# Four loads moved in time or to another queue, and attention sums moved to GpSimd, in an attention kernel with two dense layers

## The chip, the cores and the metric

The kernel runs on one core of a Trainium2 chip. The metric is the device time of one execution in microseconds (us); lower is better. The core has a matrix engine (TensorE, PE in the profile, with its weight loads as PEld), VectorE (DVE), ScalarE (ACT), GpSimd (POOL) and SyncE (SP), which here only issues transfers. Transfers run on 16 DMA engines that the core's queues share.

## What is computed

```python
a = np.exp(phi - np.max(phi, axis=2, keepdims=True))          # phi: batch 8, heads 8, seq 576, 32 memories
a = a / (np.sum(a, axis=2, keepdims=True) + 1e-09)
k_m = np.einsum('bhsm,bhsd->bhmd', a, k)                      # k, v, q: 8 x 8 x 576 x 64
v_m = np.einsum('bhsm,bhsd->bhmd', a, v)
scores = np.matmul(q, k_m.transpose(0, 1, 3, 2)) / np.sqrt(64)
scores = np.exp(scores - np.max(scores, axis=-1, keepdims=True))
attn = scores / (np.sum(scores, axis=-1, keepdims=True) + 1e-09)
x = np.matmul(attn, v_m).transpose(0, 2, 1, 3).reshape(4608, 512)
h = x @ moe_w_in                                              # 512 x 2048, weights given as float64
x = (h - np.tanh(h)) @ moe_w_out                              # 2048 x 512
h = x @ moe2_w_in
out = np.where(h > 0, h, np.exp(np.minimum(h, 0)) - 1) @ moe2_w_out
```

## The kernel before

The program is unrolled and every engine works its instructions in the order in which the Python code emits them; waits on other engines and on transfers are put in for each data dependence and for each reuse of a tile. What is emitted early on an engine and has to wait therefore holds all that is emitted behind it on that engine.

**Attention** is cut into 16 units (one batch, four heads). `Attention.unit` (line 108) is a generator; each `yield` ends a stage. In the order of its stages: maximum of phi over the sequence (119), its transpose and spread (122 to 131), the subtraction (132), exp into `a` (137), the sum of `a` over its six chunks (140, VectorE), matmuls of `a` with k and v into `km` together with the sums (147, 150), transposes of q (171), scores (192), their maximum, exp and sum (197 to 204), the normalising product (205), a transpose into `pT` (208), a split into a high and a low float part `phl` (212, 213), and a store of the result, called P, to DRAM (219). `eng` is VectorE for units 0 and 1 and GpSimd for the others. Stages also issue the next unit's loads (98 to 105) on SyncE's queue.

**Weights** come as float64. `conv` (511) loads one quarter of a weight block (512 KB, tile `raw`, two buffers) by SyncE's queue, and one stage later `convert` takes |w| of the high words on ScalarE (48, into one PSUM buffer), then two and two operations on VectorE (50, 51 and 54, 55), a copy on ScalarE (58) and a difference on GpSimd (60). Weights of layer 2 are then stored to DRAM as float32 pairs (539).

**`Staged`** runs such generators side by side: `round()` starts a waiting generator when its time has come and takes one stage of each live one, older ones first. `units` holds the attention units (one starts every six rounds), `cv` the conversions (one every two or three rounds). `need()` (507) takes rounds of `cv` at once until a weight is there.

**The stages of the program.** First (line 576) rounds of `units`, and from round 9 also of `cv`, until units 0 and 1 are done. Then 64 blocks (665) of layer 1: a block is one group of 288 tokens for one quarter of the hidden width, with two steps (`i` = 0, 1). A step emits `h_unit` (12 matmuls that read P and `vw`, 318), `g_a` (four ScalarE operations, 329 to 332), `g_b` (GpSimd 337, VectorE 338), `g_d` of the step before (350, 351), stores of finished x (378), one `x_unit` (12 matmuls, 363, and a copy to an x tile, 370 or 372), a round of `cv` and one of `units`, in every fourth block the products `vw` (303 to 308), a second `x_unit`, `g_c` (VectorE 343, 344), and a second round of `units` (in blocks 0 to 6, 28 and 29 also of `cv`). At the top of a block, P of the next block is loaded from DRAM by SyncE's queue into one of two buffers (711, 290). Layer 2 (72 groups of work on lines 419 and 456) follows and keeps its weights on the chip.

The lines that matter here, as the profile numbers them:

## Time and profile before

| | us |
|---|---|
| median of three runs (1793.1 to 1796.35) | 1793.4 |
| the profiled execution | 1789.79 |
| its span, from first to last instruction | 1787.6 |

| engine | busy us | share of the span |
|---|---|---|
| PE | 1613.6 | 90% |
| PEld | 1483.2 | 83% |
| DVE | 1255.0 | 70% |
| ACT | 959.1 | 54% |
| POOL | 763.8 | 43% |

The mean granted clock of TensorE is 0.973 of full speed. A busy share is an average over stages with different limits; the rows below are therefore cut by stage. Blocks begin at about 78 us, units are done at about 453 us, layer 1 ends at about 985 us.

### The profile page before, as it was taken

The numbers are of one execution on the slowest core, as the hardware profiler recorded it, in microseconds if no ns is written. First come the engines' busy times: TensorE is split into PE (matmuls) and PEld (weight loads), VectorE is DVE, ScalarE is ACT, GpSimd is POOL, SyncE is SP. The second block draws the span as 40 slices with busy tenths as digits, with TensorE's granted clock in tenths as the row PEclk, the third lists the DMA queues.
The fourth block names the chain that finished last, engine by engine and source line by source line (L and its number), as shares of the span: only waits on it lengthen the run. The fifth ranks groups of instructions, "written<-read, shape, count | busy, mean of one in ns | idle before, by whom it ended". The sixth has DMA issues, their size and how long they took to land.

```text
span 1787.6 us, 30091 instructions
## 1 busy us (share of the span) xinstructions
PE 1613.6 (90%) x11496; PEld 1483.2 (83%) x11496; DVE 1255.0 (70%) x1805; ACT 959.1 (54%) x1713; POOL 763.8 (43%) x539
## 2 busy tenths in 40 slices
PE   4547787888898999898999999999999999999998
PEld 2336777778897999898999999999999999999997
DVE  5859887988788998888875555555555555555554
ACT  2436776777887887787875333333333333333332
POOL 2235655656665665566653222222222222222222
PEclk9758999999999999999999999999999999999999
DMA  9547577675455445555557621111121121211210
GB/s 214 165 118 191 157 204 215 198 224 181 170 167 168 153 168 190 205 198 205 188 189 276 249 61 57 59 59 58 55 62 58 59 59 57 60 57 59 60 36 24
DMA packets 140934, 238.40 MB, mean 133 GB/s; under 512 B 8184, under 2 KB 102392, under 8 KB 138744
## 3 DMA queue, kind: packets, MB, share of 16 engines
q1 hardware_dynamic: 140792, 236.49, 42.5%
q8 instruction: 91, 1.49, 0.4%
q14 instruction: 51, 0.42, 0.1%
HBM read 159.78 MB, written 75.50 MB: 132 GB/s over the span
## 4 chain that ended last, share of the span: by engine, by line
PE 62%; DVE 13%; DMA 12%; ACT 6%; issue 5%; POOL 2%; SPq 1%; DVEq 0%; ACTq 0%; POOLq 0%
PE h_ps L419 23%; PE o_ps L456 22%; PE x_ps L363 9%; PE h_ps L318 5%; DMA p<-p_dram 5%; DMA raw<-in_moe_w_in_dram 2%; DVE s L343 2%; DVE vw L308 2%; DMA q<-in_q_dram 1%; DMA raw<-in_moe_w_out_dram 1%; DVE h_ps L338 1%; DMA x_dram<-x 1%; ACT t L329 1%; PE vw_ps L303 1%; POOL g L351 1%
## 5 line engine op out<-in xcount | busy, mean ns | idle before, releaser
L363 PE MATMUL x_ps<-g,w 128*128 128x288 f32 x3072 | 448.7, 299 | 40.3 <-DVE vw L308 16.7
L363 PEld LDWEIGHTS x_ps<-g,w 128*128 128x128 f32 x3072 | 422.3, 190 | 52.1 <-ACT x L370 14.7
L419 PEld LDWEIGHTS h_ps<-x,wi 128*128 128x128 f32 x3456 | 429.7, 190 | 11.7
L445 POOL TENSOR_TENSOR e<-hm,e 128x512 fp32r<-128x512 f32 x144 | 186.5, 1295 | 587.3 <-ACT e L444 443.3
L419 PE MATMUL h_ps<-x,wi 128*128 128x256 f32 x3456 | 433.2, 281 | 0.0
L456 PE MATMUL o_ps<-wo,e 128*128 128x512 f32 x1728 | 423.8, 394 | 0.7 <-POOL e L445 0.7
L456 PEld LDWEIGHTS o_ps<-wo,e 128*128 128x128 f32 x1728 | 314.8, 188 | 65.0 <-POOL e L445 1.1
L430 ACT ACTIVATE t_ps<-hm 128x512 f32<-128x512 f32 x144 | 86.7, 602 | 514.3 <-DVE hm L429 514.3
L337 POOL TENSOR_TENSOR v<-t,u 128x576 f32<-128x576 f32 x128 | 183.2, 1431 | 269.2 <-ACT u L330 221.6
L318 PE MATMUL h_ps<-p,vw 128*128 128x288 f32 x1536 | 236.6, 304 | 28.4 <-DMA p<-p_dram 25.2
L318 PEld LDWEIGHTS h_ps<-p,vw 128*128 128x128 f32 x1536 | 217.1, 194 | 33.0 <-issue 24.0
L436 DVE SCALAR_TENSOR_TENSOR hm<-hm,t_ps 128x512 f32<-128x512 f32 x144 | 99.0, 688 | 200.6 <-ACT hm L431 200.6
L351 POOL TENSOR_TENSOR g<-s,g 128x576 fp32r<-128x576 f32 x128 | 183.9, 1437 | 77.0 <-ACT g L350 69.5
L429 DVE TENSOR_SCALAR hm<-h_ps 128x512 f32<-128x512 f32 x144 | 99.6, 692 | 139.0 <-PE h_ps L419 139.0
L343 DVE SCALAR_TENSOR_TENSOR s<-s,v 128x576 f32<-128x576 f32 x128 | 156.5, 1223 | 0.8 <-POOL v L337 0.7
L329 ACT ACTIVATE t<-h_ps 128x576 f32<-128x576 f32 x128 | 83.0, 648 | 90.6 <-issue 43.0
L338 DVE TENSOR_TENSOR h_ps<-h_ps,t 128x576 f32<-128x576 f32 x128 | 98.3, 768 | 35.4 <-ACT u L330 34.4
L344 DVE COPY_PREDICATED s<-big,h_ps 128x576 f32<-128x576 uint32 x128 | 106.6, 833 | 11.0
L308 DVE TENSOR_TENSOR vw<-vw_ps,vw 64x512 fp32r<-64x512 f32 x128 | 88.0, 687 | 36.5 <-ACT vw L306 34.4
L332 ACT ACTIVATE big<-u,bias 128x576 f32<-128x576 f32 x128 | 98.1, 767 | 11.4 <-DVE s L344 11.2
L438 DVE TENSOR_TENSOR hm<-hm,h_ps 128x512 f32<-128x512 f32 x144 | 99.0, 687 | 5.0
L437 DVE SCALAR_TENSOR_TENSOR hm<-hm,t_ps 128x512 f32<-128x512 f32 x144 | 99.0, 687 | 5.0
(86 smaller groups left out, 1776.1 us busy)
## 6 DMA issues: line engine op xcount, KB each, us to landing
x_dram<-x SPq DMA_DIRECT2D x128, 288.0 KB
xr<-x_dram SPq DMA_DIRECT2D x72, 512.0 KB
p<-p_dram SPq DMA_DIRECT2D x62, 576.0 KB
raw<-in_moe_w_in_dram SPq DMA_DIRECT2D x32, 512.0 KB
raw<-in_moe_w_out_dram SPq DMA_DIRECT2D x32, 512.0 KB
w_dram<-wst SPq DMA_DIRECT2D x32, 512.0 KB
kv<-in_k_dram SPq DMA_DIRECT2D x16, 576.0 KB
kv<-in_v_dram SPq DMA_DIRECT2D x16, 576.0 KB
```

What stands on the lines that cost most here:

```text
L308: nc.vector.tensor_tensor(lo, src, r32(hi), op=ALU.subtract)
L318: nc.tensor.matmul(ps[:, j, :NB], lhsT=vw[a][:, kc, 128 * j:128 * j + 128], rhs=p[:, kc, b, :], start=(k == 0), stop=(k == 5))
L329: nc.scalar.activation(t, w[0], ACTF.Tanh)
L337: nc.gpsimd.tensor_tensor(v, t, u, op=ALU.mult)
L338: nc.vector.tensor_tensor(h, h, t, op=ALU.subtract)
L343: nc.vector.scalar_tensor_tensor(s, s, G_B, v, op0=ALU.add, op1=ALU.mult)
L344: nc.vector.copy_predicated(s, big.bitcast(U32), d)
L351: nc.gpsimd.tensor_tensor(g[:, 1], s, r32(g[:, 0]), op=ALU.subtract)
L363: nc.tensor.matmul(ps, lhsT=wo[pg][:, a, j, 128 * dm:128 * dm + 128], rhs=g[:, b, j, :], start=(k == 0), stop=(k == 11))
L419: nc.tensor.matmul(ps[:, j], lhsT=w3[:, a, kc, 128 * j:128 * j + 128], rhs=x[:, b, kc, :], start=(k == 0), stop=(k == 11))
L445: nc.gpsimd.tensor_tensor(e[:, 1], hm, r32(e[:, 0]), op=ALU.subtract)
L456: nc.tensor.matmul(self.acc[n][tg], lhsT=e[:, a, j, 128 * tg:128 * tg + 128], rhs=w4[:, b, j, :], start=(pg == 0 and j == 0 and i == 0), s ...
```

## The change

- P is loaded two blocks ahead by ScalarE's queue, in the second step of a block between `g_a` and `g_b`, if the units it comes from are done by then; if not, at the top of the block before its own by SyncE's queue, as it was.
- x tiles have four buffers in place of three, `raw` three in place of two; `s` of the gate has two in place of three, the conversions' `a` two in place of three, the small attention tiles two in place of three. `dmax` takes the place of `pT`, and the partial sums of `a` that of `phl`.
- The sum of `a` over its six chunks is three GpSimd additions (384, 128 and 128 elements per partition) in place of one VectorE reduction. The normalising product and the low part of P of units 0 and 1 are also on GpSimd now.
- The first three weight quarters are loaded right behind the loads of units 0 and 1 and converted three rounds apart; `cv` rounds begin at round 7, units 2 and 3 start one round later.
- A later conversion is loaded two rounds earlier ahead of its |w|, and |w| is emitted on its own, by `half()`, after `g_c` or at the start of the next round.

```diff
@@ -73,7 +73,7 @@
         pool = lambda name, n: ctx.enter_context(
             tc.tile_pool(name=name + side, bufs=n, side=side, reuse_waits="tile"))
         self.wk = pool("at_wk", 1)
-        self.sm = pool("at_sm", 3)
+        self.sm = pool("at_sm", 2)
         self.sc_p = pool("at_sc", 2 if side == "left" else 1)
         self.ps = psum
         self.q_p = pool("at_q", 2)
@@ -122,7 +122,7 @@
         nc.tensor.transpose(mT, cmax.rearrange("p h m -> p (h m)"), ident[:96, :96])
         nmax = sm.tile([128, 1], F32, tag="nmax", name="nmax")
         nc.vector.tensor_reduce(nmax, mT, axis=AX.X, op=ALU.max)
-        dmax = wk.tile([128, 128], F32, tag="dmax", name="dmax")
+        dmax = wk.tile([128, S], F32, tag="pT", name="dmax")[:, :128]
         nc.vector.tensor_scalar(dmax, ident, nmax, None, op0=ALU.mult)
         yield
         bmax = ps_tile([96, 4, M], "bmax")
@@ -137,7 +137,11 @@
         nc.scalar.activation(a[:96].rearrange("p c h m -> p h c m"), ph, ACTF.Exp)
         self.load(nxt, "phi")
         yield
-        nc.vector.tensor_reduce(asum[:96], a[:96].rearrange("p c h m -> p h m c"), axis=AX.X, op=ALU.add)
+        part = r32(wk.tile([128, 2, 2, NB], F32R, tag="phl", name="asum3")).rearrange("p r t s -> p (r t s)")
+        part = part[:96, :12 * M].rearrange("p (c h m) -> p c h m", c=3, h=4)
+        nc.gpsimd.tensor_tensor(part, a[:96, 0:3], a[:96, 3:6], op=ALU.add)
+        nc.gpsimd.tensor_tensor(part[:, 0], part[:, 0], part[:, 1], op=ALU.add)
+        nc.gpsimd.tensor_tensor(asum[:96], part[:, 0], part[:, 2], op=ALU.add)
         yield
         self.loaded.pop((u, "kv"))
         km = ps_tile([128, 2 * D + 2], "km")
@@ -202,7 +206,7 @@
         nc.vector.tensor_reduce(smax, s, axis=AX.X, op=ALU.add)
         nc.vector.tensor_scalar(smax, smax, GUARD, None, op0=ALU.add)
         nc.vector.reciprocal(smax, smax)
-        eng.tensor_tensor(s, s, smax.to_broadcast([128, 18, M]), op=ALU.mult)
+        nc.gpsimd.tensor_tensor(s, s, smax.to_broadcast([128, 18, M]), op=ALU.mult)
         yield
         pT = wk.tile([128, S], F32, tag="pT", name="pT")
         nc.vector.transpose(pT, s.rearrange("p j m -> p (j m)"))
@@ -210,7 +214,7 @@
         phl = wk.tile([128, 2, 2, NB], F32R, tag="phl", name="phl")
         pTv = pT.rearrange("p (r s) -> p r s", r=2)
         nc.scalar.activation(phl[:, :, 0], pTv, ACTF.Copy)
-        eng.tensor_tensor(phl[:, :, 1], pTv, r32(phl[:, :, 0]), op=ALU.subtract)
+        nc.gpsimd.tensor_tensor(phl[:, :, 1], pTv, r32(phl[:, :, 0]), op=ALU.subtract)
         yield
         for c, t in enumerate(first_p or ()):
             for hq in range(2):
@@ -242,12 +246,13 @@
     def __init__(self, gens=(), every=1):
         self.todo, self.live, self.every, self.wait = deque(gens), [], every, 0
         self.timed, self.rounds = deque(), 0
-        self.first = deque()
+        self.first, self.apart = deque(), []
 
     def at(self, rnd, gen):
         self.timed.append((rnd, gen))
 
     def round(self):
+        self.half()
         while self.timed and self.timed[0][0] <= self.rounds:
             self.live.append(self.timed.popleft()[1])
         self.rounds += 1
@@ -256,9 +261,18 @@
         if self.wait <= 0 and (self.first or self.todo):
             self.live.append((self.first or self.todo).popleft())
             self.wait = self.every
-        for g in list(self.live):
+        self.step([g for g in self.live if g not in self.apart])
+
+    def half(self):
+
+        gens, self.apart = self.apart, []
+        self.step(gens)
+
+    def step(self, gens):
+        for g in gens:
             try:
-                next(g)
+                if next(g):
+                    self.apart.append(g)
             except StopIteration:
                 self.live.remove(g)
 
@@ -274,9 +288,9 @@
         self.tc, self.nc, self.const = tc, tc.nc, const
         self.p_dram, self.x2_dram = p_dram, x2_dram
         pool = lambda name, n, **kw: ctx.enter_context(tc.tile_pool(name=name, bufs=n, reuse_waits="tile", **kw))
-        self.x_p = pool("x2", 3)
+        self.x_p = pool("x2", 4)
         self.g_p = pool("g", 5)
-        self.gw, self.gw1 = pool("gw", 3), pool("gw1", 1)
+        self.gw, self.gw1 = pool("gw", 2), pool("gw1", 1)
         self.p_p = pool("p", 2)
         self.vw_p = pool("vw", 1)
         self.vw, self.p, self.g, self.x2, self.work, self.x2_pool = {}, {}, {}, {}, {}, {}
@@ -285,9 +299,9 @@
         self.p[sw, n] = self.p_p.tile([128, 2, 2, NB], F32R, tag="p", name="p")
         return self.p[sw, n]
 
-    def load_p(self, sw, n):
+    def load_p(self, sw, n, queue):
         t = self.new_p(sw, n)
-        self.nc.sync.dma_start(out=r32(t).rearrange("p r t s -> p (r t s)"),
+        queue.dma_start(out=r32(t).rearrange("p r t s -> p (r t s)"),
                                in_=self.p_dram[n // 2, :, :, n % 2].rearrange("g q m f -> (g q) m f"))
 
     def vw_half(self, vm, wi, pg, po, pars=(0, 1)):
@@ -492,8 +506,8 @@
         m1 = Moe1(tc, l1a, const, p_dram, x2_dram)
         wt_p = {0: new(l1b, "wt0", 1, side="right")}
         vm_p = new(l1b, "vm", 2, side="right")
-        cv_p = new(l1b, "cv", 3, side="right")
-        raw_p = new(l1b, "raw", 2, side="right")
+        cv_p = new(l1b, "cv", 2, side="right")
+        raw_p = new(l1b, "raw", 3, side="right")
         wst_p = []
         misc = m1.misc = new(top, "ps_m", 3, space=PSUM)
         cv_ps = new(top, "ps_c", 1, space=PSUM)
@@ -508,7 +522,7 @@
             while not all((1, kind, pg, c) in converted for c in range(2)):
                 cv.round()
 
-        def conv(layer, kind, pg, c):
+        def conv(layer, kind, pg, c, lead=2):
 
             w = {("i", 1): w1, ("o", 1): w2, ("i", 2): w3, ("o", 2): w4}[kind, layer]
             raw = raw_p.tile([128, 512], mybir.dt.int64, tag="raw", name="raw")
@@ -518,7 +532,8 @@
             else:
                 r0 = 256 * pg + 128 * c
                 nc.sync.dma_start(out=raw, in_=w[r0:r0 + 128, :])
-            yield
+            for k in range(lead + 1):
+                yield k == lead
             staged = []
 
             def dst():
@@ -551,11 +566,15 @@
         at0.p_done = at1.p_done = p_done = set()
         new_vm(0)
         nc.vector.memset(r32(vm[0]), 0.0)
-        cv = Staged(conv_l1("i", 0, 1) + conv_l1("o", 0, 1), 2)
         for what in "phi", "kv", "q0", "q1":
             at0.load(0, what)
             at1.load(1, what)
-        cv.round()
+        cv_first = [conv(1, "i", k // 2, k % 2, 0) for k in range(3)]
+        cv = Staged([conv(1, "i", 1, 1)] + conv_l1("o", 0, 1), 2)
+        cv.wait = 7
+        for k, g in enumerate(cv_first):
+            next(g)
+            cv.at(3 * k, g)
 
         def unit(u):
             if u % 4 == 0 and u:
@@ -569,13 +588,13 @@
 
         first_p = [m1.new_p(0, n) for n in range(2)]
         units = Staged()
-        for u, t in ((0, 0), (1, 1), (2, 8), (3, 9)):
+        for u, t in ((0, 0), (1, 1), (2, 9), (3, 10)):
             units.at(t, unit(u))
         for u in range(4, 2 * B):
             units.at(19 + 6 * (u - 4), unit(u))
         while 1 not in p_done:
             units.round()
-            if units.rounds >= 9:
+            if units.rounds >= 7:
                 cv.round()
         pro.close()
         m1.ps_h = new(ps_h_ctx, "ps_h", 2, space=PSUM)
@@ -708,11 +727,16 @@
             if ss == 1 and j == 1 and sub == 1 and bp + 1 < B // 2 or bi == 29:
                 load_vm((bp + 1) % (B // 2))
             if nxt and nxt not in m1.p:
-                m1.load_p(*nxt)
+                m1.load_p(*nxt, nc.sync)
             for i in range(2):
                 pg = 2 * sw + i
                 m1.h_unit(sw, n, pg)
                 m1.g_a(n, pg)
+                if i == 1 and bi + 2 < len(blocks):
+                    a_ss, a_bp, a_sub, a_j = blocks[bi + 2]
+                    after = (2 * a_ss + a_sub, 4 * a_bp + a_j)
+                    if all(u in p_done for u in range(2 * (after[1] // 2) + 2)):
+                        m1.load_p(*after, nc.scalar)
                 m1.g_b(n, pg)
                 if pend:
                     m1.g_d(*pend.pop())
@@ -732,8 +756,10 @@
                     soon.popleft()()
                 x_next(bi < 22)
                 m1.g_c(n, pg)
+                cv.half()
                 if bi < 7 or 28 <= bi < 30:
                     cv.round()
+                    cv.half()
                 units.round()
                 if vw_next:
                     m1.vw_half(vm[vbp], wi[vpg + i], vpg + i, 1, pars)
```

## Rows read from the trace of the kernel before

**Rows 1.** Stage windows: length, engines' busy us (instructions), granted clock, DMA share, GB/s.

```profile
147.00:501.00 354.00, 298.21 (x2554) 271.01 (x2553) 298.31 (x442) 260.29 (x506) 205.94 (x139) 0.97 0.64 191
...
501.00:985.00 484.00, 445.38 (x3275) 437.55 (x3274) 402.23 (x558) 372.30 (x642) 291.53 (x202) 0.99 0.57 192
...
985.00:1788.00 803.00, 797.11 (x5083) 721.07 (x5081) 457.11 (x633) 273.17 (x459) 224.03 (x159) 1.00 0.21 66
```

**Rows 2.** Waits: who waited for whom: us in total, times, longest.

```profile
ACT cv_m L48 <- DMA raw<-in_moe_w_in_dram: 30.4, 4, 12.5
...
ACT cv_m L48 <- DMA raw<-in_moe_w_out_dram: 8.8, 2, 6.4
...
PE h_ps L318 <- DMA p<-p_dram: 25.2, 16, 5.8
...
DVE x L372 <- DMA x_dram<-x: 23.3, 14, 2.6
...
PE km L150 <- DVE asum L140: 15.9, 10, 3.6
```

**Rows 3.** Timeline, 26 to 43 us: start, length, instruction, idle before and releaser.

```profile
26.20 1.26 SPq L517 DMA_DIRECT2D raw<-in_moe_w_in_dram  x1
...
41.60 0.62 ACT L48 ACTIVATE cv_m<-raw 128x512 f32<-128x512 f32 x1 [12.46 <-DMA raw<-in_moe_w_in_dram]
...
42.60 0.29 PEld L192 LDWEIGHTS sc<-qT,kT 128*64 128x64 f32 x2 [10.48 <-ACT qT L173]
```

**Rows 4.** Timeline, 112 to 126 us.

```profile
112.30 0.67 SPq L290 DMA_DIRECT2D p<-p_dram  x1
...
113.47 0.91 SPq L517 DMA_DIRECT2D raw<-in_moe_w_in_dram  x2
...
125.59 0.62 ACT L48 ACTIVATE cv_m<-raw 128x512 f32<-128x512 f32 x1 [12.17 <-DMA raw<-in_moe_w_in_dram]
```

**Rows 5.** Timeline: the first ScalarE operation of blocks 24, 32 and 36.

```profile
501.38 0.65 ACT L329 ACTIVATE t<-h_ps 128x576 f32<-128x576 f32 x1 [0.46 <-issue]
...
598.96 0.65 ACT L329 ACTIVATE t<-h_ps 128x576 f32<-128x576 f32 x1 [0.46 <-issue]
...
642.27 0.65 ACT L329 ACTIVATE t<-h_ps 128x576 f32<-128x576 f32 x1 [0.46 <-issue]
```

**Rows 6.** Windows: blocks 32 to 35, blocks 44 to 47, and one microsecond.

```profile
599.00:642.30 43.30, 41.73 (x315) 41.31 (x314) 40.25 (x57) 37.37 (x65) 28.93 (x20) 1.00 0.47 159
...
735.60:781.60 46.00, 42.17 (x314) 41.36 (x313) 39.74 (x57) 37.22 (x64) 28.87 (x20) 1.00 0.59 205
...
621.00:622.00 1.00, 1.00 (x9) 1.00 (x8) 0.97 (x3) 0.70 (x2) 0.52 (x1) 1.00 0.24 97
```

**Rows 7.** Line 290, its issue times, and the timeline of one late P.

```profile
L290 SPq DMA_DIRECT2D p<-p_dram x62: 531/538/811, 112.3 to 934.2; - x62
...
660.31 0.79 SPq L290 DMA_DIRECT2D p<-p_dram  x1
...
671.98 0.58 PE L318 MATMUL h_ps<-p,vw 128*128 128x288 f32 x1 [2.26 <-DMA p<-p_dram]
```

**Rows 8.** Groups by form (busy us, mean ns | idle before), L343's min/median/max ns.

```profile
L140 DVE TENSOR_REDUCE asum<-a 96x128 f32<-96x768 f32 x16 | 23.6, 1475 | 0.0
...
L205 POOL TENSOR_TENSOR s<-s,smax 128x576 f32<-128x576 f32 x14 | 17.8, 1269 | 11.5 <-DVE smax L204 9.4 <-DVE rs L156 2.1
...
L132 POOL TENSOR_TENSOR phi<-phi,bm 96x768 f32<-96x768 f32 x14 | 28.8, 2055 | 36.0 <-ACT bm L131 32.8 <-DVE cv_m L51 3.3
...
L205 DVE TENSOR_TENSOR s<-s,smax 128x576 f32<-128x576 f32 x2 | 1.5, 758 | 0.1
...
L343 DVE SCALAR_TENSOR_TENSOR s<-s,v x128: 736/1258/2395, 81.8 to 961.0; 128x576 f32<-128x576 f32 x128
```

**Rows 9.** ScalarE's last gate operation, and line 378's issue times (min/median/max ns).

```profile
L332 ACT ACTIVATE big<-u,bias 128x576 f32<-128x576 f32 x128 | 98.1, 767 | 11.4 <-DVE s L344 11.2
...
L378 SPq DMA_DIRECT2D x_dram<-x x128: 354/365/3339, 150.7 to 977.7; - x128
```

## What the change should do to the time

> **What bounds the kernel now.** I first cut the span into stages, because the busy shares of the page are an average. In layer 2 the matrix engine works 797 of 803 us [rows 1]; the change touches nothing there, so all that can move lies in the first 985 us. In blocks 2 to 23 (147 to 501 us) no engine is full: PE and DVE are each busy 84% of the time (298 of 354 us), and 16% goes to waits. In blocks 24 to 63 PE is busy 92% (445 of 484 us).
>
> Then I read the waits [rows 2] for those that the change names, and the timeline for where they lie. ScalarE waited 39.2 us in six places for the float64 weights of a conversion (30.4 + 8.8). Two of the six are 12 us long and stop everything: the weights issued at 26.20 us reach ScalarE at 41.60, and PE, idle for 10.48 us, waits for a ScalarE copy queued behind that |w| [rows 3]; the pair issued at 113.47 ends a wait of 12.17 us at 125.59 [rows 4]. PE waited 25.2 us in 16 places for P, and VectorE 23.3 us in 14 places for a free x tile.
>
> Last I measured the block. From the start of block 32 to that of block 36 are 642.27 - 598.96 = 43.3 us [rows 5], in which PE is busy 41.7 [rows 6]; I take this for the floor that PE sets for four blocks. Blocks 44 to 47 take 46.0 for the same matmuls. The eight blocks from 24 take 501.38 to 598.96, 97.6 us, against 86.6 at the floor. What differs is the transfers: a DMA share of 0.59 in place of 0.47 [rows 6]. P of block 38 was issued at 660.31 and PE could begin only at 671.98 [rows 7], 11.7 us later, while a block lasts 43.3 / 4 = 10.8.
>
> One row explains why P is slow. While P alone is moving, the DMA share is 0.24 at 97 GB/s [rows 6]: P runs on a quarter of the engines, four of 16. Its 590 KB (128 rows of 4608 bytes) take 590 / 97 = 6.1 us of each of those four. For blocks 44 to 47 I work out an estimate: all engines together are busy 0.59 x 46.0 x 16 = 434 us, four loads of P take 4 x 4 x 6.1 = 98 of it, the other 336 spread over 16 engines are 21.0 each, so the four engines have 21.0 + 24.4 = 45.4 us of work in 46.0. Likewise blocks 32 to 35 give 38.7 of 43.3, and blocks 2 to 23 (22 loads, share 0.64 of 354) give 193 + 134 = 327 of 354.
>
> **The change part by part.** I count gains against the profiled execution (1789.8 us; span 1787.6, so 2.2 lie around it).
>
> *First weights early.* The wait of rows 3 exists since the second quarter is issued at 26.20, behind eight loads of units 2 and 3. Now three quarters go out ahead of those. PE got back 10.48 there; the bytes do not shrink, k and v of units 2 and 3 land some 1.0 MB later (two more quarters at about 240 GB/s, an estimate, 4 us), and the first |w| now stands earlier, so that it may itself wait 1 to 3 us. I take **7 us**, bounds 3 and 10.5.
>
> *Products of units 0 and 1 to GpSimd, sums of a there too, in the prologue.* DVE loses four operations of 0.758 and, for units 2 and 3, two sums of 1.475 [rows 8], 6.0 us. On GpSimd a product takes 1.27, so each step of a unit's own chain is 0.5 us longer. I count half, **3 us**, bounds -2 and 6. Units 2 and 3 start one round later and block 1 must force one more round: **-1 us**.
>
> *|w| issued apart, two rounds more lead.* At 113 us the lead is spent: block 1 needs the first output weights and takes three rounds of conversions at once, in which the new load's two rounds pass; and its transfer still stands behind P of block 2, issued at 112.30 after a wait for the store of unit 3 (it cannot go early, since unit 3 is not done). But one x unit, its copy and some GpSimd work now come ahead of that |w|. I take **5 us** of the 12.17, bounds 0 and 12. The other four waits, 39.2 - 12.46 - 12.17 = 14.6 us, lie in ordinary steps, where two rounds are two steps of about 5 to 8 us; with the one step that it had, that is more than the 15 us that the load of rows 3 took. I take **9 us**, since part of such a wait is not PE's, bounds 4 and 14.6. The |w| stands behind `g_c` of the same step and ahead of the next `t`; only the VectorE operations of a later round read it. This costs nothing as long as the weights are there; if not, `t` of the next step waits instead, as now.
>
> *Sum of a on GpSimd.* Units 5 to 15 have it in the blocks: VectorE loses 11 x 1.475 = 16 us. GpSimd gains three additions of 384, 128 and 128 elements. None is in the trace: by the elements of L205 (576 in 1.27) they are 640 / 576 x 1.27 = 1.4 us, as three whole L205 they are 3.8; since L132 (768) and L205 (576) differ about as their sizes, with a rest for contention, I take 1.6. The sum stands ahead of the next step's `v` on GpSimd, so `v`, and behind it `g`, is put off by up to 1.6; PE, which waited 15.9 us for the sum [rows 2], now waits for GpSimd. Bounds: -9 (PE and `v` pay 0.8 each time) and 16; I take **9 us**.
>
> What speaks against it is in the durations of L343, which reads two SBUF tiles: 0.74 us at best, 1.26 in the middle, 2.40 at worst [rows 8], with the same 576 elements. The Trainium skill, page "SBUF — State Buffer", section "SBUF: two separate sides", says that such a VectorE operation and a GpSimd operation share a port pair under an exclusive lock, so that the later one waits for the whole of the other. The spread agrees with that. By the rule at its hardest, every sum would hold an L343 for 1.6 us, 11 x 1.6 = 18 us lost against 16 won, and the total below would be 11 us smaller.
>
> *P two blocks ahead on ScalarE, x on four tiles.* P is now issued about 1.5 blocks, some 15 us, ahead of its use, and no longer stands behind a weight store, a weight load and their waits; 11.7 us fit into that. So the 25.2 us of PE's waits go, and most of the 23.3 of VectorE's, which lie inside the same long blocks and are not added. What is late next are the four engines: the floor of a group such as blocks 44 to 47 is not 43.3 but near 45.4. In the six groups of blocks 36 to 59 I take 1.1 us each, between 0.6 and 2.7 and nearer the DMA's: **7 us** (bounds 3 and 16). Blocks 24 to 31 have 11.0 us over the floor; blocks 28 and 29 do two conversions' rounds per step and keep theirs on VectorE, and one of the weights' waits is counted above: **4 us** (bounds 0 and 8).
>
> *Its price on ScalarE.* An issue takes 0.53 to 0.81 us of SyncE's time [rows 7], and some 60 move to ScalarE, 32 us if all were exposed. It stands right behind `big`, 0.767 us [rows 9], which the engine can work on while the sequencer issues; it waits for nothing, as `t` of that step has already waited for the last reader of the buffer. I take 0.05 each, **-3 us**, bounds 0 and -32.
>
> *At nothing:* two instead of three `s`, `a` and small tiles (the older tile's last reader is emitted a round or a step before), `dmax` in place of `pT` (its last reader, GpSimd's low part of the unit three before, is emitted one round earlier; if GpSimd lags, VectorE waits up to one such operation, 12 times 1.3 us), partial sums in place of `phl` (its store is emitted four rounds earlier).
>
> Sum: 7 + 3 - 1 + 5 + 9 + 9 + 7 + 4 - 3 = 40 us. 1789.8 - 40 = 1749.8 for an execution like the profiled one, which lies 3.6 below the median of the runs: **1753 us**.
>
> **The rivals.**
> *The four engines hold the time.* If they are really full, blocks 2 to 23 give 6 in place of 18 and blocks 24 to 59 give 3 in place of 11; with the prologue's 14 and -3 that is 20 us, 1773. For it: 45.4 of 46.0 and 327 of 354. Against it: before block 24 PE hardly waits for P at all. The Trainium skill, page "DMA: Bandwidth & Descriptors", section "Issuing engines are not separate DMA queues", says that transfers from any queue run on the same 16 engines and a second queue only saves issue time; by that rule only the earlier issue counts, which points to this rival. Chance 0.17.
> *ScalarE pays for the issue.* SyncE's stores of x take up to 3.34 us to issue while the queue is full [rows 9]. If an issue on ScalarE were held like that, `g`, the x copies and the next `t` behind it would all be late. The gains without its price are 43 us, so it turns the sign above 0.72 us per issue; at 1.2 us the kernel takes 1793.4 + 72 - 43 = 1822. Against it: P's own issues never took more than 0.81. Chance 0.07.
> *The lead does not do what it says.* Forced rounds use it up and both long waits stay in part: 4 in place of 7, 0 in place of 5, 2 in place of 9, so 25 us, 1768. Chance 0.09.
> *Both floors give way.* With two queues the four engines waste less, every group comes to 43.3, and the two long stalls go entirely: 16 + 8 in place of 11, 22 in place of 14, 28 in place of 18, so 71 us, 1722. Chance 0.09.
>
> **How the numbers follow.** The forecast, 1753 with 1738 to 1767 as its own range, has 0.58. For 8 in 10 I take in the four engines and the lost lead on one side and reach to the greater gain on the other: 1722 to 1780. The measurement can tell 0.2%, 3.6 us, from no change. Faster by more: the forecast, both smaller gains and the greater one less some mishap, 0.88; within it 0.05; slower 0.07.
>
> **What would show it.** In the profile after: no ScalarE wait of 10 us at 30 to 42 us, and the first h matmuls some 10 us earlier; a rest of the wait near 113 us; PE's wait for P near nothing; groups of four blocks at 44 to 45 us, the DMA share of these higher than 0.59; the issue on ScalarE about 0.55 us long with no gap behind it; PE's wait for the sum now on GpSimd, no longer in all than 15.9. The prediction is wrong if those waits are gone and the span is not, or if L343's median grows by more than 0.2 us, or if `t` waits where it did not.

## The result and the profile after

The changed kernel is slower: 1807.6 us median (1800.6 to 1813.2, six runs) against 1794.6 (1792.6 to 1799.8) for the kernel before, a ratio of 1.0068 with a 95% interval of 1.0042 to 1.0095. Its profiled execution took 1810.5 us with a span of 1808.7; the profiled one of before took 1789.8, so the stretches below add up to a loss of some 20 us, and the medians to 13. In the profile after, lines above 140 have moved: L304 issues P (L290 before), L332 is the h matmul (L318), L343 is `t` (L329), L357 is the VectorE operation that was L343, L386 the x copy (L372), and L142 to L144 are the three additions.

First the stretches from block to block: 2 to 24, 24 to 36, 36 to 62. The columns are those of [rows 1].

```profile
140.40:515.20 374.80, 310.31 (x2553) 281.76 (x2553) 284.37 (x430) 258.95 (x505) 222.22 (x169) 0.95 0.60 178
515.20:661.30 146.10, 130.60 (x938) 126.48 (x937) 128.35 (x177) 114.03 (x196) 91.22 (x62) 0.98 0.47 157
661.30:951.80 290.50, 273.35 (x2018) 269.01 (x2017) 257.41 (x351) 236.46 (x407) 188.36 (x128) 0.99 0.59 199
```

The same stretches of the kernel before:

```profile
146.90:501.40 354.50, 298.71 (x2559) 271.51 (x2557) 298.81 (x442) 260.41 (x507) 205.94 (x139) 0.97 0.64 191
501.40:642.30 140.90, 128.23 (x939) 126.38 (x938) 125.13 (x177) 114.00 (x197) 88.76 (x62) 0.98 0.50 162
642.30:939.40 297.10, 274.08 (x2018) 269.01 (x2017) 251.14 (x349) 235.34 (x406) 184.97 (x128) 0.99 0.57 194
```

Block 2 starts 6.5 us earlier (140.4 against 146.9). Then blocks 2 to 24 lose 20.3 us and blocks 24 to 36 lose 5.2; blocks 36 to 62 win 6.6, and block 62 alone gives 7.7 back (20.7 against 13.0). VectorE lost 14 us of work in blocks 2 to 24 (298.8 to 284.4), near the 16 that the forecast took off it, and the stretch became longer all the same. (Not all of the 14 is the sum's: e1 below, which has it back on VectorE, works 289.2 there.) PE's idle time in it rose by 8.7 us (55.8 to 64.5), and its busy time by 11.6 for the same matmuls (some records are missing), at a granted clock of 0.95 instead of 0.97.

The waits of the kernel after (us in total, times, longest), which answer to [rows 2]:

```profile
ACT cv_m L48 <- DVE cv_a L55: 52.7, 31, 4.8
POOL s L209 <- DVE smax L208: 46.0, 11, 6.1
DVE vm L191 <- ACT vm L190: 34.6, 14, 3.5
ACT phl L216 <- POOL asum L144: 26.8, 8, 4.4
...
PE km L154 <- POOL asum L144: 21.8, 13, 3.0
PE h_ps L332 <- DMA p<-p_dram: 16.5, 9, 8.1
ACT cv_m L48 <- DMA raw<-in_moe_w_in_dram: 15.8, 3, 6.2
```

What the change aimed at did shrink: the waits for weights went from 39.2 us in six places to 15.8 in three, the wait for P from 25.2 to 16.5, and VectorE's wait for an x tile is gone. Others took their place: PE waits for the sum of `a` longer than before (21.8 against 15.9), ScalarE waits 26.8 us for that sum before it may write `phl`, and GpSimd stands 46.0 us before its product `s` (46.0 in e1 too, so this one isn't the sum's).

Three places of the timeline show how. First, one sum of `a`:

```profile
356.27 1.79 POOL L60 TENSOR_TENSOR wst<-cv_a,wst 128x512 fp32r<-128x512 f32 x1
...
358.03 0.98 POOL L142 TENSOR_TENSOR asum<-a 96x384 f32<-96x384 f32 x1
...
359.09 0.45 POOL L143 TENSOR_TENSOR asum<-asum 96x128 f32<-96x128 f32 x1
359.62 0.45 POOL L144 TENSOR_TENSOR asum<-asum 96x128 f32<-96x128 f32 x1
...
360.10 0.68 ACT L216 ACTIVATE phl<-pT 128x576 fp32r<-128x576 f32 x1 [3.81 <-POOL asum L144]
...
360.12 0.24 PE L154 MATMUL km<-ones,asum 128*32 128x2 f32 x8 [2.58 <-POOL asum L144]
...
360.43 0.16 DVE L160 TENSOR_SCALAR rs<-km 128x1 f32<-128x1 f32 x1 [2.59 <-PE km L154]
...
360.82 1.49 DVE L162 TENSOR_SCALAR rm<-pmask,rs 128x2 f32<-128x2 f32 x1
...
360.86 1.43 POOL L217 TENSOR_TENSOR phl<-pT,phl 128x576 fp32r<-128x576 f32 x1 [0.80 <-DVE rs L161]
```

The additions are short, 1.88 us of work here, but they stand behind a conversion's low part, and then three engines wait at once: ScalarE 3.81 us (the partial sums lie in the tile of `phl`), PE 2.58, and VectorE 2.59 behind PE. Then VectorE is held once more: `rm` (L162), a small operation that takes 0.23 us in e1, lasts 1.49 here and ends just behind GpSimd's low part of P (L217), which the same sum had released. Second, block 28, where a step has two rounds of conversions:

```profile
568.25 0.69 DVE L55 SCALAR_TENSOR_TENSOR cv_a<-raw,cv_m 128x512 uint32<-128x512 uint32 x1
...
568.97 0.64 ACT L48 ACTIVATE cv_m<-raw 128x512 f32<-128x512 f32 x1 [4.83 <-DVE cv_a L55]
569.55 0.63 ACT L343 ACTIVATE t<-h_ps 128x576 f32<-128x576 f32 x1
```

The |w| that is issued apart needs the PSUM tile that VectorE's L55 of the conversion before it still reads. It now stands between two rounds, so ScalarE waits 4.83 us for it, with `t` behind. Block 28 takes 17.7 us instead of 12.0. Third, P of the last block:

```profile
946.72 0.46 SPq L653 DMA_DIRECT2D wi<-w_dram  x1
948.40 0.51 ACTq L304 DMA_DIRECT2D p<-p_dram  x1
950.55 0.42 SPq L653 DMA_DIRECT2D wi<-w_dram  x1
...
969.20 3.22 PE L332 MATMUL h_ps<-p,vw 128*128 128x288 f32 x12 [8.08 <-DMA p<-p_dram]
```

It was issued early and still came 20.8 us after its issue, since it moved beside the weights of layer 2.

### The profile page after: what moved, and what is told of

Same layout as the page of the kernel before. It is cut to its first block, busy times and chain, and to the rows that moved or that the text cites. A ratio compares the mean times of both kernels' runs of the same rounds, so it can differ in the third digit from the quotient of the medians.

```text
span 1808.7 us, 30153 instructions
## 1 busy us (share of the span) xinstructions
PE 1630.3 (90%) x11496; PEld 1500.1 (83%) x11496; DVE 1241.3 (69%) x1785; ACT 958.6 (53%) x1713; POOL 803.8 (44%) x591
## 3 DMA queue, kind: packets, MB, share of 16 engines
q8 instruction: 91, 1.49, 0.4%
## 4 chain that ended last, share of the span: by engine, by line
PE 59%; DMA 5%; ACT 5%; DVE 3%; issue 2%; POOL 0%; ACTq 0%; DVEq 0%; POOLq 0%
PE h_ps L433 23%; PE o_ps L470 22%; PE x_ps L377 9%; DMA p<-p_dram 5%; PE h_ps L332 5%; DVE vw L322 1%; ACT t L343 1%; ACT u L344 1%; ACT big L346 1%; DVE s L357 1%; ACT vw L320 1%; PE vw_ps L317 1%; ACT g L364 0%; ACT s L345 0%; ACT x L384 0%
## 5 line engine op out<-in xcount | busy, mean ns | idle before, releaser
L377 PE MATMUL x_ps<-g,w 128*128 128x288 f32 x3072 | 455.3, 302 | 39.2 <-DVE vw L322 18.1
L377 PEld LDWEIGHTS x_ps<-g,w 128*128 128x128 f32 x3072 | 429.1, 193 | 48.6 <-PE vw_ps L317 11.7
L433 PEld LDWEIGHTS h_ps<-x,wi 128*128 128x128 f32 x3456 | 429.8, 190 | 11.7
L332 PE MATMUL h_ps<-p,vw 128*128 128x288 f32 x1536 | 247.0, 314 | 26.4 <-DMA p<-p_dram 16.5
L332 PEld LDWEIGHTS h_ps<-p,vw 128*128 128x128 f32 x1536 | 226.3, 202 | 35.5 <-issue 22.4
L357 DVE SCALAR_TENSOR_TENSOR s<-s,v 128x576 f32<-128x576 f32 x128 | 154.4, 1206 | 2.6 <-POOL v L351 1.1
L343 ACT ACTIVATE t<-h_ps 128x576 f32<-128x576 f32 x128 | 83.3, 651 | 116.8 <-issue 55.8
L345 ACT ACTIVATE s<-u,bias 128x576 f32<-128x576 f32 x128 | 99.6, 778 | 11.6 <-ACT u L344 0.8
(86 smaller groups left out, 1797.2 us busy)
```

The source lines that it names most:

```text
L332: nc.tensor.matmul(ps[:, j, :NB], lhsT=vw[a][:, kc, 128 * j:128 * j + 128], rhs=p[:, kc, b, :], start=(k == 0), stop=(k == 5))
L343: nc.scalar.activation(t, w[0], ACTF.Tanh)
L345: nc.scalar.activation(s, u, ACTF.Square, bias=bias[:, 0:1], scale=G_S)
L357: nc.vector.scalar_tensor_tensor(s, s, G_B, v, op0=ALU.add, op1=ALU.mult)
L377: nc.tensor.matmul(ps, lhsT=wo[pg][:, a, j, 128 * dm:128 * dm + 128], rhs=g[:, b, j, :], start=(k == 0), stop=(k == 11))
L433: nc.tensor.matmul(ps[:, j], lhsT=w3[:, a, kc, 128 * j:128 * j + 128], rhs=x[:, b, kc, :], start=(k == 0), stop=(k == 11))
```

## The experiments

Every kernel was timed against the kernel before on its chip. Stretches are from profiled executions (us, from the first `t` of a block to that of another); block 0 is the time at which it starts. Short names stand for the labels below. One execution doesn't decide a few us: f3, g2 and g5 are the same program up to block 30, and their blocks 2 to 24 took 356.7, 352.6 and 354.3; after and f2 are the same up to block 0, which starts at 73.5 and 68.8. Nor do all differences of medians: by the intervals of the ratios, after and f2 differ by 11 us, give or take 6, but after and e1 by 4.5, give or take 5.6.

| kernel | median us | ratio to before, 95% | block 0 | 2 to 24 | 24 to 36 | 36 to 60 | block 60 | block 62 |
|---|---|---|---|---|---|---|---|---|
| before | 1794.6 | 1 | 77.9 | 354.5 | 140.9 | 276.7 | 9.6 | 13.0 |
| after | 1807.6 | 1.0042 to 1.0095 | 73.5 | 374.8 | 146.1 | 270.7 | 9.6 | 20.7 |
| e7: before, P on ScalarE | 1872.0 | 1.0418 to 1.0466 | 77.8 | 378.1 | 149.0 | 326.7 | 9.6 | 18.4 |
| f4: before, x tiles of after | 1798.8 | 0.9999 to 1.0035 | 79.3 | 353.3 | 142.3 | 284.1 | 9.6 | 15.3 |
| f2: after, P by SP | 1797.2 | 0.9986 to 1.0026 | 68.8 | 368.5 | 145.4 | 268.2 | 16.4 | 13.1 |
| e1: after, sum on VectorE | 1803.1 | 1.0027 to 1.0059 | 71.9 | 362.6 | 145.4 | 273.6 | 9.6 | 17.2 |
| e3: after, own tile for the sum | 1810.4 | 1.0072 to 1.0108 | 72.4 | 370.6 | 146.9 | 273.3 | 9.6 | 16.7 |
| e5: before, sum on GpSimd | 1800.4 | 0.9986 to 1.0042 | 76.8 | 369.3 | 141.4 | 281.1 | 9.6 | 15.3 |
| g1: f2 and e1 together | 1790.3 | 0.9961 to 0.9988 | 71.8 | 359.3 | 145.1 | 265.0 | 16.2 | 15.4 |
| e4: after, abs(w) in the next round | 1806.8 | 1.0047 to 1.0108 | 69.4 | 365.0 | 143.7 | 287.7 | 9.6 | 16.5 |
| e6: e4, sum on VectorE | 1800.4 | 1.0007 to 1.0058 | 71.0 | 357.4 | 141.8 | 286.1 | 9.6 | 15.0 |
| f1: e6, abs(w) apart from block 30 | 1788.5 | 0.9947 to 0.9984 | 68.3 | 357.3 | 140.5 | 277.3 | 9.6 | 15.0 |
| f3: e6, P by SP | 1796.5 | 0.9985 to 1.0015 | 69.2 | 356.7 | 142.4 | 276.7 | 16.6 | 15.9 |
| g2: f1, P by SP | 1784.6 | 0.9925 to 0.9967 | 70.2 | 352.6 | 139.3 | 270.0 | 16.2 | 14.4 |
| g4: g2, three x tiles | 1784.5 | 0.9921 to 0.9977 | 70.6 | 356.0 | 139.5 | 271.6 | 15.0 | 14.2 |
| e2: after, units at 8, 9 | 1824.4 | 1.0149 to 1.0188 | 72.8 | 383.8 | 145.3 | 272.9 | 9.6 | 21.4 |
| e8: e6, units at 8, 9 | 1829.4 | 1.0167 to 1.0220 | 74.2 | 381.7 | 141.3 | 281.6 | 9.6 | 13.8 |
| g3: f3, units at 8, 9 | 1808.7 | 1.0056 to 1.0112 | 74.1 | 369.9 | 141.0 | 281.1 | 16.8 | 13.6 |
| g5: g2, conversions a round later | 1785.2 | 0.9940 to 0.9979 | 69.8 | 354.3 | 140.3 | 270.8 | 18.5 | 14.2 |
| g6: before, the same | 1791.5 | 0.9971 to 1.0009 | 75.5 | 354.2 | 142.2 | 269.9 | 15.2 | 13.8 |

### P on ScalarE's queue (e7, f4, f2, f3)

e7 makes this one edit in the kernel before, with the x tiles that it came with:

```diff
-                m1.load_p(*nxt)
+                m1.load_p(*nxt, nc.sync)
@@ after g_a of the second step
+                if i == 1 and bi + 2 < len(blocks):
+                    ...
+                        m1.load_p(*after, nc.scalar)
```

> The kernel before with one part of the change alone: P of every block loaded through ScalarE's queue two blocks ahead, and four x tiles. Theory: blocks 36 to 61 gain 6 us as in the kernel after, block 62 loses 7 to 8 us by the P of block 63 behind the last weight loads, blocks 2 to 24 stay at 354 to 356 us: 1793 to 1798. Rival (the P loads cost time in the stages with units as well, by ScalarE's issue or by shared DMA engines): blocks 2 to 24 at 362 us or more, and 1802 or more.

It took 1872.0 us, 78 more than before. The theory was far off; the rival's bounds were met, but it looked at the stages with units (24 us), and 50 us were lost in blocks 36 to 60. Its waits for weights:

```profile
ACT cv_m L48 <- DMA raw<-in_moe_w_in_dram: 72.1, 10, 11.7
ACT cv_m L48 <- DMA raw<-in_moe_w_out_dram: 42.0, 6, 8.7
```

They come to 114 us, where the kernel before had 39.2. The timeline of e7 around block 37 shows where they come from:

```profile
689.76 0.53 ACTq L290 DMA_DIRECT2D p<-p_dram  x1
689.91 0.53 SPq L539 DMA_DIRECT2D w_dram<-wst  x1
690.53 0.79 SPq L517 DMA_DIRECT2D raw<-in_moe_w_in_dram  x1
...
704.23 0.64 ACT L48 ACTIVATE cv_m<-raw 128x512 f32<-128x512 f32 x1 [7.71 <-DMA raw<-in_moe_w_in_dram]
```

The same load in the kernel before, where P follows on the same queue at 660.31 [rows 7]:

```profile
659.00 0.57 SPq L539 DMA_DIRECT2D w_dram<-wst  x1
659.67 0.55 SPq L517 DMA_DIRECT2D raw<-in_moe_w_in_dram  x1
...
665.71 0.64 ACT L48 ACTIVATE cv_m<-raw 128x512 f32<-128x512 f32 x1 [0.36 <-DVE x L372]
```

Before, the weights of the next conversion were there at most 6.0 us after their issue, ahead of P. In e7 they are released 13.7 us after it; P, the store and the load move at the same time, and P sits on four of the 16 engines. It is a pattern: the nine weight loads of blocks 37 to 55 that were issued 0.8 us behind P reached ScalarE after 12.3 to 13.7 us, and none of the ten that were issued 2.5 us or more ahead of the nearest P was waited for. No run without the longer lead has P ahead of the load on one queue, so the second queue and this order aren't told apart. One microsecond of e7 shows what is left at the end, a quarter of the engines busy while ScalarE already waits:

```profile
699.00:700.00 1.00, 1.00 (x10) 1.00 (x9) 0.29 (x1) 0.00 (x0) 0.52 (x1) 1.00 0.25 95
```

f4 keeps the x tiles (four, and two `gw` tiles) and leaves P with SP.

```diff
-        self.x_p = pool("x2", 3)
+        self.x_p = pool("x2", 4)
-        self.gw, self.gw1 = pool("gw", 3), pool("gw1", 1)
+        self.gw, self.gw1 = pool("gw", 2), pool("gw1", 1)
```

> The kernel before with four x tiles instead of three and two gw tiles instead of three, nothing else. The kernel before with P on ScalarE's queue (and these tiles) took 1872 us. Theory: what cost 78 us there is P beside the weight loads on the same DMA engines, with 72 and 42 us of waits for weights: so here 1786 to 1796, blocks 36 to 62 at 290 to 298, and waits for weights no longer than in the kernel before (39 us). Rival (two gw tiles, or x tiles that let other transfers run ahead, are the cost): 1830 or more, with weights waited for longer.

1798.8 us: the tiles are not what cost 78 us. They gave no gain either; the x wait is gone, and blocks 36 to 60 are 7 us longer. The time lies between the two expectations, far from the rival's.

f2 is the kernel after with every P by SP, one block ahead.

```diff
-                if i == 1 and bi + 2 < len(blocks):
+                if i == 2 and bi + 2 < len(blocks):
```

> The kernel after with every P loaded by SP one block ahead, as before the change; all its other parts stay, the four x tiles too. Theory: the 6 us of blocks 36 to 62 come from P and |w| together, so that stretch goes back from 290 to 295 to 299 us, block 62 from 20.7 to about 13, blocks 2 to 24 stay at 368 to 376, as P's queue costs nothing there: 1801 to 1808. Rival (P through ScalarE's queue costs time beside the units, as in the kernel before with P alone, where blocks 2 to 24 took 378): blocks 2 to 24 at 364 or less, and 1797 or less.

1797.2 us, 10 us less than after: less than the theory had, and blocks 2 to 24 (368.5) above the rival's 364. In blocks 36 to 60 P by SP is no slower (268.2 against 270.7), so the gain that the kernel after has there isn't P's. f3 makes the same edit in e6.

> The kernel with |w| in the next round and the sum of a on VectorE (1800.4 us), with every P by SP one block ahead: of the change only the early first weights with their lead and third buffer, the four x tiles and the two products on GpSimd are left. Theory: P on ScalarE's queue runs beside the weight load and the store on the same DMA engines and makes both late when all are issued together; with P behind the weight on SP's queue blocks 36 to 62 fall from 307 to 293 to 298 us, blocks 2 to 24 stay at 355 to 360: 1784 to 1792. Rival (the collision isn't it, the new rounds of the conversions are): blocks 36 to 62 stay at 304 or more, 1797 or more.

1796.5 against 1800.4, and 276.7 against 286.1 us in blocks 36 to 60; block 60 hid most of it in the stretch to block 62 that I had named, and the time is 4.5 us over the theory's. In block 60 P by SP stands behind the last weight's store and is late (16.6 us against 9.6), the one place where ScalarE's queue helps. Five pairs differ in P's queue alone or nearly so (after and f2, e1 and g1, e6 and f3, e8 and g3, f1 and g2): blocks 36 to 60 are 0.5 to 9.4 us shorter with SP in all five, and the medians 3.9 to 20.7 us lower.

### The sum of `a` on GpSimd (e1, e3, e5, g1)

e1 takes the three additions out of the kernel after.

```diff
-        nc.gpsimd.tensor_tensor(part, a[:96, 0:3], a[:96, 3:6], op=ALU.add)
-        ...
+        nc.vector.tensor_reduce(asum[:96], a[:96].rearrange("p c h m -> p h m c"), axis=AX.X, op=ALU.add)
```

> The changed kernel with one part undone: the sum of a over its chunks is one VectorE reduction again; all else as changed, the extra forced round of units included. From the start of block 2 to that of block 24 the kernel before took 354.5 us (146.9 to 501.4) and the changed one 374.8 (140.4 to 515.2). Theory S (the sum on GpSimd comes late and holds PE, and ScalarE through the tile that it shares with the high and low parts of P): this stretch falls to 355 to 360, the whole by 15 to 20 us. Rival R (the round by which units 2 and 3 start later shifts every unit's stages by half a step against the blocks): it stays at 370 or more.

1803.1 us, 4.5 less, and blocks 2 to 24 are 12.2 us shorter, between the two expectations: the wait for `asum` before `phl` (26.8 us) and GpSimd's part in PE's wait are gone. So is the hold on `rm`, as its min/median/max in after, e1 and e5 (below) show:

```profile
L162 DVE TENSOR_SCALAR rm<-pmask,rs x16: 228/1271/1495, 15.7 to 421.8; 128x2 f32<-128x2 f32 x16
...
L158 DVE TENSOR_SCALAR rm<-pmask,rs x16: 228/229/1072, 15.9 to 416.6; 128x2 f32<-128x2 f32 x16
...
L162 DVE TENSOR_SCALAR rm<-pmask,rs x16: 228/1631/3395, 15.7 to 416.1; 128x2 f32<-128x2 f32 x16
```

In blocks 2 to 24 it takes 12.9 us in after and 2.3 in e1, for ten operations each. Every long one ends some 0.03 us behind a GpSimd operation that overlaps it; in e5 it is up to three of these in a row. e3 gives the partial sums a tile of their own (and takes the fourth x tile for the room).

```diff
-        part = r32(wk.tile([128, 2, 2, NB], F32R, tag="phl", name="asum3"))...
+        part = wk.tile([96, 3, 4, M], F32, tag="part", name="asum3")
```

> The changed kernel with the partial sums of a in a tile of their own (and three x tiles for the room; x tiles are waited for only after 480 us). Theory S1 (ScalarE's copy into the high part of P waits for GpSimd's last sum because of the shared tile, 26.8 us in 8 waits, and all behind it on ScalarE with it): blocks 2 to 23 fall by 12 us or more. Theory S2 (PE waits for the sum, shared tile or not): they fall by under 5 us. R: no change.

4.2 us less in blocks 2 to 24, within what executions differ by, and no less in all: the shared tile is at most the smaller part (S2). e5 puts the sum on GpSimd in the kernel before.

> The kernel before with one part of the change alone: the sum of a as three GpSimd additions in the shared tile. Units start as before, so their stages fall as before. Theory S: blocks 2 to 23 rise from 354.5 to 365 or more, the whole by 10 us or more. Theory R, or S only together with the shifted half step: 350 to 358, the whole within 5 us of before or below it.

1800.4 us, not to be told from before by its interval (runs from 1785 to 1807); no gain of 9 us. The profiled execution, its slowest, has 369.3 us in blocks 2 to 24, as theory S; `rm` takes 25.0 us there against 4.1 in before. g1 takes the sum back where P is SP's too.

> The kernel after with every P by SP one block ahead (1797.2 us) and the sum of a on VectorE too. Theory: the sum on GpSimd costs 4 to 6 us of the time wherever it was undone (1807.6 to 1803.1, 1806.8 to 1800.4), so 1789 to 1793, with blocks 2 to 24 falling from 368.5 to 355 to 360 us and blocks 36 to 62 at 293 to 297. Rival (the sum costs only beside P on ScalarE's queue): 1796 or more, blocks 2 to 24 at 365 or more.

1790.3 us, 6.9 below f2 (by the ratios 5.7, give or take 4.3), as the theory had it.

### |w| issued apart (e4, e6, f1)

e4 is the kernel after with |w| in the next round, and P of block 63 by SP.

```diff
-                yield k == lead
+                yield
-                if i == 1 and bi + 2 < len(blocks):
+                if i == 1 and bi + 3 < len(blocks):
```

> The kernel after, with two edits: |w| of a conversion goes back into the next ordinary round (the two spare rounds of lead stay), and the P of block 63, the last, is loaded by SP again, one block ahead. Theory: the |w| put between two rounds stands right behind VectorE's work on the conversion before it wherever a step has two rounds (blocks 0 to 6, 28, 29); that cost 6.5 us in blocks 28 and 29 and part of blocks 2 to 6, and the late P of block 63 cost 7.7 us in block 62. So block 28 falls from 17.75 to about 12.0 us, block 29 from 16.46 to about 15.7, block 62 from 20.7 to about 13.0, the ScalarE waits of conversions for cv_a in blocks 2 to 24 fall from 17 to about 4 us, that stretch from 375 to about 367, and the time from 1807.6 to about 1786 to 1794. Rival (the extra forced round shifts the stages of the units, and that costs the time, not the |w|): blocks 2 to 24 stay at 373 or more, and only blocks 28, 29 and 62 are regained: 1793 to 1796 at best, with blocks 2 to 24 unchanged.

Blocks 28 and 29 fell to 12.1 and 12.3 us and blocks 2 to 24 by 9.8, as forecast. But blocks 36 to 60 rose from 270.7 to 287.7, block 62 fell to 16.5 only, and the time stayed at 1806.8: |w| apart costs where rounds crowd; behind block 30 its return cost time, but there it also moved |w| to the other half of the block (below). e6 has the sum on VectorE too.

> The kernel before the last expectation's (|w| in the next round, P of block 63 by SP), and with it the sum of a on VectorE again. What is left of the change: first weights early with a lead of two rounds and three raw buffers, P through ScalarE's queue but for the last block, four x tiles, GpSimd for the two products of the left lane. Theory: the sum on GpSimd is worth 4.5 us (kernel after 1807.6, the same with the sum on VectorE 1803.1), so 1781 to 1789, faster than the kernel before, with blocks 2 to 24 at 354 to 358 us. Rival (P on ScalarE or the shifted stages cost time in blocks 2 to 24): that stretch stays at 362 or more, and the time at 1790 or more.

1800.4, slower than expected for the same 286 us in blocks 36 to 60. So f1 issues |w| apart only for conversions begun from block 30 on.

```diff
+            own = len(apart_on) > 0
             for k in range(lead + 1):
-                yield
+                yield k == lead and own
@@ in the loop over blocks
+            if bi == 30:
+                apart_on.append(1)
+                cv.wait += 1
```

> The kernel with |w| in the next round, P of block 63 by SP and the sum of a on VectorE (1800.4 us, 357 us in blocks 2 to 24, 307 us in blocks 36 to 62), with |w| apart again for conversions begun from block 30 on. Theory: |w| apart costs where conversions or units crowd (blocks 2 to 30) and is what P on ScalarE's queue needs afterwards, since the weight load then leaves ahead of P and the store of the weight before it behind, instead of all three at once: blocks 2 to 24 stay at 357, blocks 36 to 62 fall from 307 to 290 to 295, the time is 1783 to 1790, under the kernel before. Rival (blocks 36 to 62 are slower there for the phase that the units left the conversions in, whatever |w| does): blocks 36 to 62 stay over 302, the time at 1797 or more.

1788.5 us, the first that is faster than before. Blocks 36 to 60 came back to 277.3, not to the 270.7 of after. g2 gives P to SP as well.

> The kernel with |w| apart from block 30 on, the sum of a on VectorE and P on ScalarE's queue but for the last block (1788.5 us, under the kernel before), now with every P by SP one block ahead. Theory: P on ScalarE's queue costs 4 to 10 us wherever it was undone beside a lead of two rounds (1807.6 to 1797.2, 1800.4 to 1796.5): 1780 to 1786. Rival (behind |w| apart P on ScalarE's queue gains, as its 290.5 against 294.8 us in blocks 36 to 62 says): 1789 or more, blocks 36 to 62 at 302 or more.

1784.6 us, ratio 0.9946 (0.9925 to 0.9967): faster than both kernels. Its stretches 2 to 24, 24 to 36 and 36 to 60:

```profile
142.10:494.70 352.60, 299.11 (x2551) 272.33 (x2549) 288.50 (x437) 256.73 (x504) 201.64 (x138) 0.98 0.63 191
494.70:633.90 139.20, 128.19 (x938) 126.24 (x938) 126.29 (x178) 113.76 (x196) 88.74 (x62) 0.98 0.52 162
633.90:903.90 270.00, 256.54 (x1874) 251.77 (x1873) 243.62 (x335) 221.34 (x384) 174.50 (x121) 0.99 0.59 194
```

In blocks 2 to 24 the matmuls are back at 299 us, with a clock of 0.98. (In f3, the same program up to block 30, they took 303.6 at 0.96.) g4 is g2 with three x and three `gw` tiles.

> The kernel with |w| apart from block 30 on, the sum of a on VectorE and every P by SP, with three x tiles and three gw tiles as before the change. Theory: the four x tiles took the wait for x (16 us in blocks 36 to 62) away and gave it back as later P and weights (the kernel before with four took 303 us there instead of 297, 1798.8 in all): so within 4 us of the same kernel with four, or faster. Rival (beside the lead they are worth their 7 us): 6 us or more slower than with four.

1784.5 us: four x tiles with two `gw` are worth no more than three of each.

### The rounds of the units, and the half of the block (e2, e8, g3, g5, g6)

e2, e8 and g3 put units 2 and 3 back to rounds 8 and 9, in the kernel after, in e6 and in f3.

```diff
-        for u, t in ((0, 0), (1, 1), (2, 9), (3, 10)):
+        for u, t in ((0, 0), (1, 1), (2, 8), (3, 9)):
```

> The changed kernel with units 2 and 3 started at rounds 8 and 9 as before, so that five and not six rounds are forced in block 1 and every later stage of a unit falls into the other half of its step; the sum of a stays on GpSimd. Theory R: blocks 2 to 23 fall from 374.8 to 360 or less. Theory S: they stay at 370 or more. If both are needed, the sum on GpSimd being late only in the half of a step in which v, the low part of g and a conversion stand ahead of it: 355 to 362 here, and about the same in the run with the sum on VectorE.

> The kernel with |w| in the next round, P of block 63 by SP and the sum of a on VectorE, and with units 2 and 3 at rounds 8 and 9 as before the change. With the sum and the |w| as before, it asks what the shift of the units by one round costs. Theory: the shift alone is worth little: within 4 us of the same kernel without this edit. Rival (the shift by half a step costs): 5 us or more faster than it, blocks 2 to 24 back at 355.

> The kernel with |w| in the next round, the sum of a on VectorE and every P by SP (1796.5 us), with units 2 and 3 at rounds 8 and 9 as before the change. Beside P on ScalarE's queue this edit cost 29 us (1800.4 to 1829.4). Theory: P on ScalarE's queue is what costs in that phase too (the kernel before, at rounds 8 and 9, lost 78 us by it, 24 of them in blocks 2 to 24), so with P by SP the edit is worth little: 1792 to 1800, blocks 2 to 24 at 352 to 360. Rival (rounds 8 and 9 suit only the lead of before, whatever P does): 1810 or more, blocks 2 to 24 at 368 or more.

All three are slower, by 16.8, 29.0 and 12.2 us, mostly in blocks 2 to 24: the shift of the units is needed beside the earlier weights, and P on ScalarE's queue accounts for some of its price only. Why, these runs don't settle.

The last two ask what gave blocks 36 to 62 their gain. In after, f2, e1 and g1 the |w| runs in the second step of a block, in before, e4, e6 and f3 in the first. Both kernels begin the conversions from block 30 on one round later (`cv.wait += 2` instead of 1 in g2; `cv.wait += 1` in before).

> The kernel with |w| apart from block 30 on, the sum of a on VectorE and every P by SP (1784.6 us, blocks 36 to 62 in 300.3), with the conversions from block 30 on begun one more round later, so that their |w| runs in the second step of a block instead of the first. Theory: which half of the block the conversions take sets the 7 us of blocks 36 to 62, not P: that stretch falls to 291 to 296, the time to 1775 to 1781. Rival (it is the rounds of the whole kernel after, or chance): 298 or more there, and 1783 or more.

> The kernel before with one edit: the conversions from block 30 on begin one round later, so that their |w| runs in the second step of a block. P, tiles, lead and sums stay as before. Theory (the half of the block alone is the cause): blocks 36 to 62 take 290 to 295 us instead of 297.1, the time is 1788 to 1792. Rival (it takes the |w| apart, with its lead, as well): 297 or more there, and 1793 or more.

In the kernel before, blocks 36 to 60 fell from 276.7 to 269.9 us by this alone, as much as the kernel after had won, with P where it was, and PE's wait for P there from 12.4 us to nothing; the part below on the prediction shows what the move did to P. In g2 it gave nothing (270.0 and 270.8), and there the wait for P was 5.4 us to begin with. In all 20 kernels blocks 36 to 60 take 265 to 274 us where |w| runs in the second step, and 276.7 or more where it runs in the first, but for g2 and g4 (270.0, 271.6). In g5 and g6 the conversions end a round later, and then P of block 61 is late behind the last weight's store, as in this timeline of g5:

```profile
904.18 3.76 SPq L553 DMA_DIRECT2D w_dram<-wst  x2
908.04 0.56 SPq L300 DMA_DIRECT2D p<-p_dram  x1
...
921.39 3.10 PE L328 MATMUL h_ps<-p,vw 128*128 128x288 f32 x12 [7.67 <-DMA p<-p_dram]
```

So g6 is at 1791.5, within the measurement of before.

## Why the prediction was wrong

The forecast was 40 us of gain, 1753 us in a range of 1722 to 1780; the measured change is a loss of 13. The condition that it named for this came true: the waits are shorter and the span isn't; so did another, `t` waiting where it did not (block 28). The waits stood where the prediction put them, and most of them went. What failed is the reason given for P's wait, and the pricing of what takes the place of the others.

**P two blocks ahead on ScalarE's queue: 11 us of gain forecast, a loss of 10.4 measured (f2).** Two steps failed. The first is "P is now issued about 1.5 blocks, some 15 us, ahead of its use". P has two buffers, and a load waits until the last h matmul that reads its buffer has ended. For one P each, in before (660.31; block 39's, not block 38's as the prediction has it), after and g6:

```profile
654.80 1.77 PE L318 MATMUL h_ps<-p,vw 128*128 128x288 f32 x12
...
659.00 0.57 SPq L539 DMA_DIRECT2D w_dram<-wst  x1
...
660.31 0.79 SPq L290 DMA_DIRECT2D p<-p_dram  x1
```

```profile
664.26 1.77 PE L332 MATMUL h_ps<-p,vw 128*128 128x288 f32 x12
...
668.13 0.53 ACTq L304 DMA_DIRECT2D p<-p_dram  x1
```

```profile
654.55 1.77 PE L318 MATMUL h_ps<-p,vw 128*128 128x288 f32 x12
...
656.35 0.54 SPq L290 DMA_DIRECT2D p<-p_dram  x1
...
662.96 0.57 SPq L539 DMA_DIRECT2D w_dram<-wst  x1
```

In before the buffer is free at 656.57, but SyncE's queue stands at the weight's store, which waits for GpSimd (line 60), and P follows 3.7 us late. In after ScalarE issues it 2.1 us late, behind the operations of `g_a`. In g6, where the store comes in the other half of the block, SyncE issues it at once. Over the 24 loads of blocks 36 to 59 the median delay is 3.1 us in before, 1.8 in after and 0.03 in f2 and g6, and P is issued 13.8, 13.5, 15.9 and 14.4 us ahead of its first use. So "two blocks ahead" was hardly earlier than one block ahead had been. What cost P in before was the place behind the store: g6, which moves the store, has none of the 12.4 us that PE waits for P in blocks 36 to 60 of before.

The second is "what is late next are the four engines": it counted P's own lateness only. In before the weights go ahead of P; in e7 they move beside it and take 13.7 us instead of at most 6.0. The lead of two rounds covers most of that: e8, which has it, needs 281.6 us for blocks 36 to 60 where e7 needs 326.7 (it has the early weights and the GpSimd products as well), and in after the shortest time from a weight load to its |w| behind block 36 is 13.9 us. So after loses 10 and e7 78; where the 10 lie is shown only in part, by PE's wait for P, 16.5 us against 11.7 in f2. The 45.4 us that the prediction works out for a group is near the mean of six in after (45.1) by luck: these last 43.2 to 46.5 at DMA shares from 0.48 to 0.61, and g1 does a group in 43.9 in which the same working gives the four engines 46.0:

```profile
824.70:868.60 43.90, 42.05 (x314) 41.36 (x313) 40.45 (x57) 37.31 (x64) 29.47 (x20) 1.00 0.63 218
```

The 6 us that blocks 36 to 60 won looked like this term and weren't: P by SP keeps them (f2, g1), and g6 has them without anything of the change.

The first rival cited the Trainium skill, page "DMA: Bandwidth & Descriptors", section "Issuing engines are not separate DMA queues": transfers from any queue run on the same 16 engines. The traces agree: in e7 P on ScalarE's queue delayed weights on SyncE's (13.7 us against at most 6.0). But the rival took the rule for a smaller gain, where it was a loss. **ScalarE's issue** cost next to nothing, as forecast: 514 ns at least, 515 in the middle, 1102 at most, 61 times. The only rival for slower had the wrong mechanism.

**Sum of `a` on GpSimd: 9 us of gain forecast, a loss of 4.5 to 6.9 (e1, g1; only the second is clear of noise).** The work was estimated at 1.6 us and took 1.19 + 0.58 + 0.45 = 2.2 in the mean. The failed step is the queue: "The sum stands ahead of the next step's `v`" looked at what stands behind the sum, not at what stands ahead of it. The lower bound, -9, was the nearer one, and its reason, that PE then waits for GpSimd, was the right one. The median of the old L343 stayed at 1258 ns, but that doesn't clear the rule that spoke against it, since 11 sums can't move the median of 128. The lock on the shared port pair, of which the Trainium skill (page "SBUF — State Buffer", section "SBUF: two separate sides") says that the later of two operations that need the pair waits for the whole of the other, agrees with the rows of another operation: `rm`, 0.23 us alone, is held to the end of GpSimd's, 10.6 us more in blocks 2 to 24 of after than in e1. So of the 15.1 us that the ten sums take on VectorE in e1, 4.8 were saved (284.4 us of work against 289.2). How much of it reached the time isn't separated from the waits. Of the edits "at nothing", the partial sums in place of `phl` were wrong: I had looked at the store of the old `phl`, but the next `phl` waits for the sum, 26.8 us in eight places, at most some 4 us of blocks 2 to 24 (e3).

**|w| apart: "nothing as long as the weights are there".** Wrong in blocks with two rounds per step: the weights were there, and VectorE's last operation on the conversion before was not. It shows in a wait that stands beside those of [rows 2] in the same view, 41.9 us before and 52.7 after, which I hadn't read since the change doesn't name it:

```profile
ACT cv_m L48 <- DVE cv_a L55: 41.9, 30, 7.2
```

Taking |w| apart away up to block 30 is worth 5.7 us (g1 to g2; by the ratios 5.0, give or take 4.5).

**The waits for weights: right as waits, not as time.** The 14.6 us of the four ordinary ones are gone, and no stretch got shorter by 9; blocks 2 to 24 have too many other waits of like length.

**The prologue: nearly right.** Block 0 starts at 68.3 to 74.2 us in the 15 kernels with early weights (median 71.0) and at 75.5 to 79.3 in the five without (77.8), so 6.8 us of the 10 forecast for its first two terms. The wait near 113 us fell from 12.17 to 6.24, at 121.81. The four x tiles took the x wait and gave nothing (f4, g4).

That leaves a sum that can be followed along one order of the edits: of the loss of 13 us, P is 10.4 (f2), the sum 6.9 (g1), |w| apart ahead of block 30 5.7 (g2), 23 in all; what stays of the change (early weights, lead, two products on GpSimd, |w| apart later) gains the 10 us by which g2 is faster than before. In another order (e4, e6, f3) |w| gives 0.8, the sum 6.4 and P 3.9, so the parts depend on each other. Open are why rounds 8 and 9 cost so much beside the lead, and where most of P's 10 us lie.

## What to carry to other kernels

Before a load is emitted earlier, look when its buffer comes free: with two buffers, two blocks ahead was the same moment as one. A queue is also an order: before a transfer is moved to a queue of its own, list what it stood behind and what stood behind it, and ask what happens to those when all move at once on the same engines. Work moved to an idle engine is paid by its place in that engine's queue, so read what stands ahead of it at the time it is needed, and who waits for it, not its length. And a stretch that got faster isn't proof of the part that was meant for it; take that part out alone.

## What the runs showed of the hardware

- Beside a load of 128 rows of 4608 bytes, which ran on four of the 16 DMA engines, and a store, a weight load issued 0.8 us behind it on another queue took 13.7 us instead of at most 6.0 (nine of these 12.3 to 13.7); in the last microseconds only a quarter of the engines were busy (0.25, 95 GB/s).
- A DMA issue on ScalarE's queue took 0.515 us in the middle and left no gap on ScalarE; by the DMA packets the transfer had landed 8.8 to 14.7 us later beside ordinary traffic, and PE got it 20.8 us after its issue beside the weights of layer 2.
- A VectorE operation of 0.23 us (`rm`, 128x2) lasted 1.47 to 1.50 us in eight of ten places of after, each time to some 0.03 us behind the end of a GpSimd operation; in e5 up to 3.4 us, behind three GpSimd operations in a row.
- In blocks 2 to 24 the same matmuls (2550 to 2559 records) took PE 297 to 310 us in 20 profiled executions, at granted clocks of 0.93 to 0.98. More waiting doesn't always go with it: g3 had PE idle for 69.3 us and busy for 300.6, after idle for 64.5 and busy for 310.3; f3 and g2, the same program there, were idle for 53 us and busy for 303.6 at 0.96 and 299.1 at 0.98. No term of the forecast held this spread.
